# Moving Pool's sums, weight loads and mask operations in a fused attention and FFN block

## Chip, cores and metric

The kernel runs on one core of one Trainium2 chip. The metric is the device time of one execution in microseconds (us), as the median of several executions. Single executions of one kernel mostly agree to about 0.3%. The trace of a run is of one execution, which need not be a typical one.

TensorE is called PE, VectorE DVE, ScalarE ACT and GpSimd Pool. SP is the engine that here only issues DMA transfers, in program order.

## The reference

A pre-norm linear attention block is followed by a pre-norm gated FFN, on 2048 tokens of width 1024, in bf16:

```python
h  = x + A(layernorm(x))         # A: wqkv (1024 x 3072), 32 heads of 32
                                 # phi(t) = where(t > 0, t+1, exp(t)) + 1e-6
                                 # kv = sum_s phi(k) v ;  z = sum_s phi(k)
                                 # o = phi(q) kv / (phi(q) z + 1e-6) ;  out = o @ wo
h2 = h + B(layernorm(h))         # B: (relu(x Wg) * (x Wu)) @ Wd, F = 3584
```

## The kernel before

A token tile is 128 tokens, so there are 16. The program has four stretches:

1. **K and V, to about 140 us.** LN of each x tile, then k, v and their running product kv. From tile 4 on the products use Strassen's scheme with seven products in place of eight, which needs sums of weight blocks. Pool makes 32 of those: 16 for the V weights, then 16 for the Q weights.
2. **Q groups, 140 to 194 us.** In the first of them the kv sums are masked by head ("KV masks").
3. **Token tiles, 194 to 266 us.** For each tile: numerator `num`, quotient `o`, a DMA transpose of o, the o-projection, `h`, a store of h, LN on ACT and Pool, a DMA transpose of the normalized tile, and at the end four sums `S` over all eight tiles on DVE.
4. **FFN, 266 us to the end.** PE without a gap.

A buffer tracker turns every operation's reads and writes into semaphore waits, and each engine runs its operations in program order. That order is what the change alters. First, the Pool sums hang on the LN statistics: after a tile's rstd, up to three of them are issued.

```python
def ln_stats(src_full, src_chunk_bufs, name):
    # ... dve: bn_stats, bn_aggr, ve = var + eps
    PL.add("pool", lambda e: e.tensor_tensor(out=rstd[:, k, :], in0=ve[:, k, :], in1=neghalf[:], op=ALU.pow), ...)

def ln1_stats(st):
    ln1_k[st] = ln_stats(x1[:, i, :], B_x1[i], "ln1_%d" % st)
    for _ in range(min(3, len(pool_q))):
        pool_q.pop(0)()               # weight sums: TWv (16), then TWq (16)
```

The token tiles come from this loop. `a4` is the o-projection with h, the store of h and the first half of LN; `a4_norm` is LN's last step on ACT with the transpose; `a2` is numerator, quotient and the transpose of o.

```python
for _ in range(NWG):                  # NWG = 6
    load_w_next()                     # 512 KB of FFN weights each
LAG = NE                              # 4
for t in range(NE, NST + LAG + 1):
    if LAG + 1 <= t < TPP + LAG + 1:
        a4_norm(t - LAG - 1)          # ACT: xn = norm ; SP: transpose xn -> hnT
    if LAG <= t < NST + LAG:
        a4(t - LAG)                   # PE: o @ wo ; DVE: h ; SP: load x, store h
                                      # ACT, Pool: mean, variance, rstd (tiles 0 to 7)
    if t < NST:
        a2(t)                         # PE: num ; DVE: o = num / den ; SP: transpose o
    if t == 8:
        for f_ in t_sums(0, "pool") + t_sums(1, "pool"):
            f_()                      # eight Pool sums in a row
    if 13 <= t < 17:
        s_sums()[t - 13]()            # DVE: S sums, read all of hnT
```

h has three buffers (`NHS = 3`): h of tile t waits until tile t-3 has been normalized and its store has been read out.

## Time and profile before

The median is 778.93 us, and the profiled execution has a span of 777.3 us. Times inside a trace count from the start of its span. In the table, the first o-projection ends the Q groups, and the last numerator product (tile 15) is the last step of the token tiles at which PE waited in this kernel.

| | before |
|---|---|
| median of 4 | 778.93 us |
| products of tiles 14 and 15 into kv (end of K and V) | 139.81 us |
| first o-projection (first recorded matmul) | 194.31 us |
| last numerator product | 251.68 us |
| from there to the end | 525.6 us |

The page says that PE is 96% busy, but that average hides the start. These are its slices of the span (40 equal ones of 19.4 us; digits are tenths of busy time, PEclk tenths of the full clock that was granted):

```profile
PE   7698999999996999999999999999999999999998
...
DVE  5789976889755698888887656756686776753343
...
PEclk9799999999998999999999999999999999999999
```

PE's gaps are in the first 13 slices. After that come the last o-projections and the FFN, and nothing in this change touches them. Next, the timeline of Pool around 20 us: start, duration, engine, line, operation, result and inputs, count, and in brackets the idle time just before with what ended it.

```profile
20.40 3.60 POOL L725 TENSOR_TENSOR RW<-RAB 128x512 f16<-128x512 bf16 x3 [8.69 <-DMA RAB<-in_A_wqkv_dram]
23.96 0.55 POOL L613 TENSOR_TENSOR rstd<-ve,neghalf 128x1 f32<-128x1 f32 x1
24.48 3.67 POOL L725 TENSOR_TENSOR RW<-RAB 128x512 f16<-128x512 bf16 x3
```

Pool stood idle for 8.69 us because its first weight sum waited for a wqkv load. The rstd of tile 3 stands behind those three sums. This wait passes down the line, as the timelines of DVE and PE show (in PE's line `ps<-ident,RXH` is the transpose of tile 3's normalized x):

```profile
24.55 1.36 DVE L619 TENSOR_SCALAR RXH<-RE,mv,rstd 128x1024 bf16<-128x1024 bf16 x1 [8.87 <-POOL rstd L613]
```
```profile
25.97 1.04 PE L675 MATMUL ps<-ident,RXH 128*128 128x128 bf16 x8 [9.28 <-DVE RXH L619]
```

The same DVE line shows a second effect: the norm took 1.36 us beside a Pool sum. Alone it takes 0.54 us, as in the timeline of DVE at 37.96 us. Two 10 us windows show the stretch on either side of this wait: from 20 us on nobody but Pool is full, and from 80 us on DVE is the full engine, not PE. Columns: window, its length, busy us (and instructions) of PE, PEld, DVE, ACT and Pool, then granted clock, DMA share and GB/s.

```profile
20.00:30.00 10.00, 4.03 (x16) 2.05 (x17) 5.32 (x8) 1.08 (x2) 9.28 (x10) 0.50 0.09 30
...
80.00:90.00 10.00, 8.77 (x52) 4.14 (x52) 9.66 (x22) 3.96 (x7) 3.43 (x4) 1.00 0.36 80
```

In the token tiles, the waits in the window from 195 to 260 us (engine, line, what it waited for, us in total, times, longest) name Pool again. The eight sums in a row kept tile 5's LN back, ACT waited 7.4 us at one place, and DVE waited 5.8 us for a free h buffer:

```profile
ACT RXH L1033 <- POOL s L1023: 17.3, 8, 7.4
...
DVE RXH L994 <- ACT RXH L1033: 5.8, 1, 5.8
```

PE's timeline shows what came of it. `RW,RE` is an o-projection (16 matmuls, about 3.5 us), `kvz,RAB` a numerator. Some records are missing, hence 15 for 16.

```profile
231.64 3.63 PE L592 MATMUL ps<-RW,RE 128*128 128x512 bf16 x16 [1.07 <-DMA RE<-RE]
237.85 0.64 PE L592 MATMUL ps<-kvz,RAB 128*128 128x132 bf16 x8 [2.59 <-DVE RE L975]
241.26 5.58 PE L592 MATMUL ps<-RW,RE 128*128 128x512 bf16 x15 [2.77 <-DMA RE<-RE]
...
251.68 0.64 PE L592 MATMUL ps<-kvz,RAB 128*128 128x132 bf16 x8 [0.92 <-DVE RE L975]
```

An undisturbed tile takes 3.92 us. The projection at 241.26 us took 5.58 us because the clock had dropped to half in the stalls (granted 0.50 from 240 to 244 us).

### The profile page before, as it was taken

Reading aid. Unit: us, or ns where it says so; the run is one execution under the profiler, and the core shown is the slowest. Engines: PE = TensorE matmul, PEld = TensorE weight load, DVE = VectorE, ACT = ScalarE, POOL = GpSimd, SP = SyncE. Lnnn points to the kernel's source line nnn. Section 1 sums busy time; section 2 is a strip of 40 time slices with the busy share of each in tenths; the row PEclk is TensorE's granted clock in tenths of the full one; section 3 lists DMA queues with packets and bytes.
Section 4 is the critical chain, followed back from the end, with each engine's and each line's share of the span. In section 5 each row is a group of like instructions: output and inputs, shape, how many; then the busy total and the mean of one; then the engine's idle time right before and its main releaser. Section 6 shows DMA issues by size and latency. Waiting matters only on the chain.

```text
span 777.3 us, 10071 instructions
## 1 busy us (share of the span) xinstructions
PE 743.3 (96%) x3544; PEld 337.6 (43%) x3599; DVE 554.2 (71%) x1104; ACT 294.4 (38%) x502; POOL 75.6 (10%) x116
## 2 busy tenths in 40 slices
PE   7698999999996999999999999999999999999998
PEld 3343444334443444444444444444444444444443
DVE  5789976889755698888887656756686776753343
ACT  3234556566644145445454200014545445421000
POOL 1776200000261000000000010000000000000000
PEclk9799999999998999999999999999999999999999
DMA  9343210401997677655543799871322313026664
GB/s 304 118 120 82 55 28 1 148 6 37 279 209 196 209 222 237 188 166 164 178 147 114 240 245 270 250 249 55 109 86 77 109 55 108 1 61 183 203 183 142
DMA packets 160226, 113.39 MB, mean 146 GB/s; under 512 B 51504, under 2 KB 141360, under 8 KB 160176
## 3 DMA queue, kind: packets, MB, share of 16 engines
q1 hardware_dynamic: 160176, 112.75, 50.4%
q8 instruction: 28, 0.46, 0.2%
q14 instruction: 22, 0.18, 0.1%
HBM read 85.46 MB, written 15.73 MB: 130 GB/s over the span
## 4 chain that ended last, share of the span: by engine, by line
PE 75%; DVE 8%; ACT 6%; POOL 5%; issue 4%; DMA 2%; SPq 0%; DVEq 0%; POOLq 0%; ACTq 0%
PE ps L592 75%; POOL RW L725 2%; ACT ps L597 1%; DVE st L605 1%; DMA RAB<-in_A_wqkv_dram 1%; POOL RO L1088 1%; ACT RX L630 1%; DVE RX L634 1%; DVE RXH L619 1%; ACT RX L1010 1%; ACT RX L1007 1%; DVE RX L826 1%; DVE RAB L637 1%; POOL rstd L613 1%; ACT RXH L597 1%
## 5 line engine op out<-in xcount | busy, mean ns | idle before, releaser
L592 PE MATMUL ps<-RC,RO 128*128 128x512 f16 x672 | 154.2, 379 | 0.0
L597 ACT ACTIVATE ps<-ps 128x512 f32<-128x512 f32 x152 | 88.7, 583 | 169.7 <-PE ps L592 158.3
L592 PE MATMUL ps<-RW,RAB 128*128 128x512 f16 (+1 forms) x685 | 151.1, 379 | 0.6
L592 PEld LDWEIGHTS ps<-RW,RAB 128*128 128x128 bf16 (+1 forms) x696 | 68.1, 98 | 82.2
L592 PE MATMUL ps<-RH,RWG 128*128 128x512 bf16 x435 | 103.0, 379 | 0.7
L592 PEld LDWEIGHTS ps<-RC,RO 128*128 128x128 f16 x672 | 65.7, 98 | 79.3
L597 ACT ACTIVATE RE<-ps 128x512 f32<-128x512 f32 x120 | 71.0, 597 | 76.7 <-PE ps L592 54.5
L592 PE MATMUL ps<-RC,RWG 128*128 128x512 f16 x296 | 70.7, 379 | 0.0
L1157 DVE TENSOR_TENSOR RAB<-ps,RAB 128x512 bf16<-128x512 f32 x28 | 19.4, 692 | 67.1 <-PE ps L592 66.8
L592 PEld LDWEIGHTS ps<-RH,RWG 128*128 128x128 bf16 x448 | 43.8, 98 | 52.9
L592 PE MATMUL ps<-RW,RE 128*128 128x512 bf16 x248 | 58.8, 389 | 5.2 <-DMA RE<-RE 4.2
L592 PE MATMUL ps<-RH,RO 128*128 128x512 bf16 (+1 forms) x242 | 58.3, 379 | 0.7
L597 ACT ACTIVATE RAB<-ps 128x512 bf16<-128x512 f32 x56 | 33.4, 597 | 62.1 <-PE ps L592 62.1
L592 PE MATMUL ps<-RAB 128*128 128x512 bf16 x215 | 53.6, 390 | 1.3 <-ACT RAB L678 0.7
L1088 DVE TENSOR_TENSOR RO<-RWG,RO 128x512 f16<-128x512 bf16 x108 | 45.4, 420 | 1.8
L592 PEld LDWEIGHTS ps<-RC,RWG 128*128 128x128 bf16 (+1 forms) x296 | 28.5, 98 | 35.7 <-ACT ps L597 2.2
L1164 DVE TENSOR_TENSOR RE<-ps,RE 128x512 f32<-128x512 f32 x56 | 38.5, 691 | 5.1 <-ACT RE L597 5.0
L613 POOL TENSOR_TENSOR rstd<-ve,neghalf 128x1 f32<-128x1 f32 x24 | 14.6, 610 | 281.6 <-DVE ve L610 281.6
L1088 DVE TENSOR_TENSOR RO<-RWG 128x512 f16<-128x512 bf16 x108 | 40.6, 417 | 0.0
L605 DVE BATCH_NORM_STATS2 st<-RE 128x6 f32<-128x512 bf16 x48 | 30.7, 681 | 13.7 <-DMA RE<-h_scr 12.8
L592 PEld LDWEIGHTS ps<-RW,RE 128*128 128x128 bf16 x256 | 24.7, 100 | 34.6 <-DMA RE<-RE 5.2
L1169 DVE TENSOR_TENSOR RE<-ps,RE 128x512 f32<-128x512 f32 x56 | 38.2, 681 | 0.0
(111 smaller groups left out, 796.3 us busy)
## 6 DMA issues: line engine op xcount, KB each, us to landing
RWG<-in_B_W_gate_dram SPq DMA_DIRECT2D x28, 512.0 KB, 3.7
RWG<-in_B_W_up_dram SPq DMA_DIRECT2D x28, 512.0 KB, 4.9
RW<-t_scr SPq DMA_DIRECT2D x56, 256.0 KB, 3.3
RW<-in_B_W_down_dram SPq DMA_DIRECT2D x42, 256.0 KB, 4.4
RE<-in_A_x_dram SPq DMA_DIRECT2D x31, 256.0 KB, 3.6
RW<-in_B_W_down_dram SPq DMA_DIRECT2D x14, 512.0 KB, 3.9
t_scr<-RW SPq DMA_DIRECT2D x14, 512.0 KB, 4.9
RAB<-in_A_wqkv_dram SPq DMA_DIRECT2D x8, 512.0 KB, 8.3
```

The source lines that it names most:

```text
L592: lambda e: e.matmul(out_ap, lhsT, rhs, start=start, stop=stop, skip_group_check=skip),
L597: PL.add("act", lambda e: e.activation(out=dst, in_=src, func=func), reads=reads, writes=writes, name=name)
L605: PL.add("dve", lambda e, c=c: e.bn_stats(out=st6[:, k, c * 6:(c + 1) * 6], in_=src_full[:, c * BCH:(c + 1) * BCH]), reads=[src_chunk_bufs ...
L613: PL.add("pool", lambda e: e.tensor_tensor(out=rstd[:, k, :], in0=ve[:, k, :], in1=neghalf[:], op=ALU.pow), reads=[B_ve[k], B_neghalf], wr ...
L619: PL.add("dve", lambda e: e.tensor_scalar(out=dst_ap, in0=src_full, scalar1=mv[:, k, 0:1], scalar2=rstd[:, k, :], op0=ALU.subtract, op1=AL ...
L630: PL.add("act", lambda e: e.activation(out=Et[:, k, :], in_=src, func=ACTF.Exp), reads=[src_buf], writes=[B_E[k]], name=name + "_exp")
L634: PL.add("dve", lambda e: e.tensor_scalar(out=Et[:, k, :], in0=Et[:, k, :], scalar1=1.0, scalar2=1e-6, op0=ALU.min, op1=ALU.add), reads=[] ...
L725: PL.add(eng, lambda e: e.tensor_tensor(out=tw(j)[:, d0:d0 + chunk, :], in0=in0(d0), in1=in1(d0), op=ALU.subtract), reads=reads, writes=[b ...
L1088: PL.add(eng, lambda e: e.tensor_tensor(out=Tring[:, k, j], in0=in0, in1=in1, op=ALU.subtract), reads=reads, writes=[B_T[k][j]], name="T%d ...
L1157: PL.add("dve", lambda e: e.tensor_tensor(out=hh[:, f1, 0:SBW], in0=bank(BA[1]), in1=r11[:, rr, :], op=ALU.mult), reads=[B_bank[BA[1]], B_ ...
L1164: PL.add("dve", lambda e, w=w: e.tensor_tensor(out=ftmp[:, 4 + w, :], in0=bank(BF_[w]), in1=ftmp[:, 2 + w, :], op=ALU.add), reads=[B_bank[ ...
L1169: PL.add("dve", lambda e, w=w: e.tensor_tensor(out=ftmp[:, 6 + w, :], in0=bank(BB[w]), in1=ftmp[:, w, :], op=ALU.add), reads=[B_bank[BB[w] ...
```

## The change

The intent has three parts. The weight sums start only at tile 5, so that no LN step stands behind a sum that waits for a load. The eight FFN sums of Pool go one per tile, and the six FFN weight loads one per tile too, from tile 5 to tile 10, so that they don't all come at once. The 24 small KV mask operations become five wide ones, two Q groups later.

```diff
         def ln1_stats(st):
             ln1_k[st] = ln_stats(x1[:, i, :], B_x1[i], "ln1_%d" % st)
-            for _ in range(min(3, len(pool_q))):
-                pool_q.pop(0)()
+            run(pool_q, {5: 5, 6: 5, 7: 3, 8: 3, 9: 2, 10: 2}.get(st, 3) if st >= 5 else 0)
 ...
         def kvfin():
-            for g in range(NG):       # 8 x: kvz[g] = kv[g] * bmask
-            for g in range(NG):       # 8 x: zsb[g] = one column of PSUM
-            for g in range(NG):       # 8 x: kvz[g, P:] = bmask4 * zsb[g]   (bodies cut)
+            for b0, nb, ng, g0 in ((0, 2, GPB, 0), (2, 1, NG - 2 * GPB, 2 * GPB)):
+                # kvm: one tensor_tensor over nb*ng groups, mask broadcast (cut)
+                # zsb: one tensor_copy over nb*ng groups (cut)
+            PL.add("dve", lambda e: e.tensor_tensor(
+                out=kvz[:, :, P:P + HPG], in0=bmask4[:].unsqueeze(1).to_broadcast([P, NG, HPG]),
+                in1=zsb[:].unsqueeze(2).to_broadcast([P, NG, HPG]), op=ALU.mult), ...)
 ...
                 if r == 0 and ct == 0:
-                    hooks[3] = lambda: (kvacc(NST - 2), kvacc(NST - 1), kvfin())
+                    hooks[3] = lambda: (kvacc(NST - 2), kvacc(NST - 1))
+                if r == 0 and ct == 2:
+                    hooks[3] = kvfin
 ...
         flush()
-        for _ in range(NWG):
-            load_w_next()
         LAG = NE
+        pool_t = t_sums(0, "pool") + t_sums(1, "pool")
         for t in range(NE, NST + LAG + 1):
             ...
-            if t == 8:
-                for f_ in t_sums(0, "pool") + t_sums(1, "pool"):
-                    f_()
+            if 5 <= t < 5 + NWG:
+                load_w_next()
+            if t >= 9:
+                run(pool_t, 1)
```

## The prediction

It was made from the kernel before, its trace and the diff alone, before the changed kernel had been built.

> **What bounds it now.** By the chain of waits, TensorE work is 75% of the 777.3 us span. From about 266 us on (the FFN) TensorE is busy throughout; the change leaves that alone. The time to win lies in the first 254 us.
>
> **1. Weight sums on Pool.** *Now:* the first three sums stand on Pool in front of tile 3's rstd and wait 8.69 us for a wqkv load (timeline of Pool, 20.40 us). VectorE waits 8.87 us for that rstd and TensorE 9.28 us for VectorE's norm; afterwards the granted clock is 0.50 (20 to 30 us). After the change no sum precedes tile 5, so this goes. But from 30 to 96 us VectorE is 95 to 98% busy in most windows and sets the pace, so the slow clock is hidden. And the sums cost VectorE: a norm takes 0.54 us alone and 1.36 us beside a Pool sum, an L634 step 0.28 against 0.6 to 1.05. The Trainium skill ("SBUF — State Buffer", Who interferes with whom) says VectorE and GpSimd share a port pair as an exclusive lock; these durations agree. I count about 12 us so lost, some 0.45 us per sum. Today 3 of the 32 sums fall in the idle gap; then all will fall in busy time, and tiles 12 to 14 get 9 instead of 2, where VectorE has little slack. Estimate: +8.9 (wait gone) + 0.8 (its inflated norm) - 1.4 (more collisions) = **8.3 us gained**.
>
> **2. KV masks.** 24 small VectorE operations take 4.3 us (140.65 to 144.9 us) in the first Q group; TensorE loses 0.76 + 0.70 us. Five wide ones, estimated from 0.69 us for 512 and 1.22 us for 1024 elements out of PSUM: 1.9 us, two groups later. **1.1 us gained.**
>
> **3. Token tiles.** *Now:* eight Pool sums (222.5 to 231.65 us) stand in front of tile 5's LN steps; ACT waits 7.4 us for Pool, VectorE 5.8 us for a free h buffer, TensorE 1.07 + 2.59 + 2.77 + 0.92 us, in part at clock 0.50. The o-projection of tile 12 starts at 252.15 us; at the undisturbed 3.92 us per tile it would be 241.4. One sum per tile fits into Pool's 2.46 us gap. But LN repeats only every 4.885 us on ACT and Pool, its transposes stand in SP's order before the next o transposes (landing 4.2 us): tile 12 can't start before about 245.2. Then VectorE's S sums wait for tile 7's transpose and hold o of tile 14: about 247.5. The six spread 512 KB weight loads take SP's issue time (0.6 to 1.4 us each) and DMA time (share above 1.0 from 198 to 230 us) from these transposes, while the idle DMA before 195 us goes unused. **4.0 us gained** (0 to 7).
>
> **Sum:** 8.3 + 1.1 + 4.0 = 13.4: **765.5 us** (1.7% less), range 760.5 to 770.5. Faster by over 2%: 0.29; within 2%: 0.69; slower: 0.02.
>
> **To check:** no TensorE wait for VectorE's norm near 17 us and no half clock there; Pool sums between 22 and 95 us, VectorE nearly full; K group of tiles 4 and 5 about 11 us earlier, shrinking to 8 by 100 us; masks under 2 us; LN every 4.9 us without the 7.4 us hole; a wait of 2 to 4 us before the last numerator product, behind the S sums.
>
> **What would make it wrong:** bursts of five sums colliding more (gain 5) or mostly with idle VectorE (gain 11); transposes queueing behind the spread loads; the second stall dropping TensorE's clock.

## The result, and the profile after

The changed kernel takes 770.81 us (770.62 to 771.08, 4 runs) against 778.93 us. The ratio is 0.9896, with a 95% interval from 0.9879 to 0.9913. Ratios are the mean time of one kernel's fast runs over that of the other's in the same rounds, so they aren't quite the ratio of the medians. The gain is 8.1 us; 13.4 were predicted. The time lies just above the range.

| | before | after | gain in this stretch |
|---|---|---|---|
| end of K and V | 139.81 | 131.79 | 8.02 |
| first o-projection | 194.31 | 184.97 | 1.32 |
| last numerator product | 251.68 | 243.40 | -1.06 |
| end of the span | 777.3 | 769.0 | 0.0 |

The first two stretches gained what was forecast (8.3 and 1.1 us). The third was to gain 4.0 us and lost one. The lines of the changed kernel are numbered 3 or 4 higher than before.

In the slices of the page, each now 19.2 us long, PE's weak start is gone from the first two slices (8 and 9 where there was 7 and 6) and DVE is fuller there. The third slice has become weaker (7 where there was 9): it holds the wait of 4.7 us for DVE shown below. At the token tiles the one dip of PE to 6 (13th slice) has become two slices of 7 (12th and 13th):

```profile
PE   8979999999977999999999999999999999999998
...
DVE  7989975889746698888886756748676686653433
...
PEclk9989999999999999999999999999999999999999
```

The timeline of Pool shows the rstd of tiles 3 and 4 free of any sum, and the first five sums behind tile 5's:

```profile
14.91 0.55 POOL L613 TENSOR_TENSOR rstd<-ve,neghalf 128x1 f32<-128x1 f32 x1 [3.15 <-DVE ve L610]
17.98 0.55 POOL L613 TENSOR_TENSOR rstd<-ve,neghalf 128x1 f32<-128x1 f32 x1 [2.53 <-DVE ve L610]
21.91 0.55 POOL L613 TENSOR_TENSOR rstd<-ve,neghalf 128x1 f32<-128x1 f32 x1 [3.38 <-DVE ve L610]
22.43 6.14 POOL L728 TENSOR_TENSOR RW<-RAB 128x512 f16<-128x512 bf16 x5
```

PE's transpose of tile 3 comes at 16.58 instead of 25.97 us, without a wait. What remains: in the table of PE's waits, the one for DVE's phi step in the K group of tiles 4 and 5 has grown from 2.2 to 4.7 us, and the largest is now for transposes of o:

```profile
PE ps L592 <- DMA RE<-RE: 8.0, 5, 3.1
PE ps L592 <- DVE RE L637: 4.7, 1, 4.7
...
PE ps L592 <- DVE RE L979: 1.4, 1, 1.4
```

The five mask operations take 1.6 us (146.76 to 148.40 us) by the timeline of DVE, where the 24 took 4.3 (140.65 to 144.92 us); first the kernel before, then the changed one:

```profile
140.65 1.67 DVE L941 TENSOR_TENSOR kvz<-ps,bmask 128x128 bf16<-128x128 f32 x8 [1.50 <-PE ps L592]
142.24 1.49 DVE L947 COPY zsb<-ps 128x1 f32<-128x1 f32 x8
143.77 1.15 DVE L950 TENSOR_SCALAR kvz<-bmask,zsb 128x4 bf16<-128x4 f32 x8
```
```profile
146.76 0.95 DVE L946 TENSOR_TENSOR kvz<-ps,bmask 128x768 bf16<-128x768 f32 x1
147.63 0.15 DVE L950 COPY zsb<-ps 128x6 f32<-128x6 f32 x1
147.70 0.41 DVE L946 TENSOR_TENSOR kvz<-ps,bmask 128x256 bf16<-128x256 f32 x1
148.03 0.15 DVE L950 COPY zsb<-ps 128x2 f32<-128x2 f32 x1
148.21 0.19 DVE L953 TENSOR_TENSOR kvz<-bmask,zsb 128x32 bf16<-128x32 f32 x1
```

In the token tiles the waits have changed their names. The longest wait of ACT for Pool is 1.4 us where it was 7.4, so the sums are indeed out of the way. Now DVE waits for the stores of h (four times, 11.2 us), PE for transposes of o, and DVE's first S sum for the last transpose of LN:

```profile
ACT RXH L1037 <- POOL s L1027: 11.4, 8, 1.4
DVE RXH L998 <- DMA h_scr<-RXH: 11.2, 4, 4.4
...
PE ps L592 <- DMA RE<-RE: 8.0, 5, 3.1
...
DVE RC L1074 <- DMA RH<-RXH: 4.7, 1, 4.7
```

SP's timeline shows where they come from. First one tile of the kernel before, then the changed kernel. Each tile has a transpose of o (`RE<-RE`), now a weight load (`RWG<-in_B_W...`), then the LN transpose (`RH<-RXH`), a load of x and a store of h. The second column is how long SP was busy issuing:

```profile
217.97 1.43 SPq L502 DMA_TRANSPOSE RE<-RE  x1
219.45 1.66 SPq L502 DMA_TRANSPOSE RH<-RXH  x1
```
```profile
221.37 1.47 SPq L502 DMA_TRANSPOSE RE<-RE  x1
222.88 0.58 SPq L498 DMA_DIRECT2D RWG<-in_B_W_gate_dram  x1
223.51 3.43 SPq L502 DMA_TRANSPOSE RH<-RXH  x1
...
228.15 1.47 SPq L502 DMA_TRANSPOSE RE<-RE  x1
229.67 0.58 SPq L498 DMA_DIRECT2D RWG<-in_B_W_up_dram  x1
230.29 2.48 SPq L502 DMA_TRANSPOSE RH<-RXH  x1
```

The LN transpose behind a weight load took 3.43 and 2.48 us to issue; before, its median was 1.35 us. Everything behind it in SP's order comes later. ACT finished tile 7's norm at 229.2 us; its transpose was issued at 235.49 us, 6.3 us later. So LN's own pace (4.885 us per tile, kept exactly) no longer set the pace of the tiles; the transfers behind SP's queue did.

### The profile page after: what moved, and what is told of

It is laid out like the page before. It is cut to its first block, busy times and chain, and to the rows that moved or that the text cites. A ratio compares the mean times of both kernels' runs of the same rounds, so it can differ in the third digit from the quotient of the medians.

```text
span 769.0 us, 10054 instructions
## 1 busy us (share of the span) xinstructions
PE 741.7 (96%) x3544; PEld 337.4 (44%) x3599; DVE 553.2 (72%) x1085; ACT 294.2 (38%) x502; POOL 75.9 (10%) x116
## 4 chain that ended last, share of the span: by engine, by line
PE 79%; DVE 8%; ACT 5%; issue 3%; DMA 2%; POOL 2%; SPq 1%; DVEq 0%; ACTq 0%; POOLq 0%
PE ps L592 79%; DVE RX L634 1%; ACT RX L1014 1%; ACT RX L1011 1%; ACT ps L597 1%; DMA RE<-in_A_x_dram 1%; DVE RE L637 1%; ACT RX L630 1%; DVE st L605 1%; DVE RX L829 1%; SPq L498 1%; DVE RAB L637 1%; DVE RC L728 1%; DMA RE<-RE 1%; DVE RXH L619 1%
## 5 line engine op out<-in xcount | busy, mean ns | idle before, releaser
L597 ACT ACTIVATE RE<-ps 128x512 f32<-128x512 f32 x120 | 71.0, 597 | 76.7 <-PE ps L592 54.5
L592 PEld LDWEIGHTS ps<-RH,RWG 128*128 128x128 bf16 x448 | 43.8, 98 | 52.9
L605 DVE BATCH_NORM_STATS2 st<-RE 128x6 f32<-128x512 bf16 x48 | 30.7, 680 | 13.9 <-DMA RE<-h_scr 12.9
```

The costliest lines, as they stand in the source:

```text
L592: lambda e: e.matmul(out_ap, lhsT, rhs, start=start, stop=stop, skip_group_check=skip),
L597: PL.add("act", lambda e: e.activation(out=dst, in_=src, func=func), reads=reads, writes=writes, name=name)
L605: PL.add("dve", lambda e, c=c: e.bn_stats(out=st6[:, k, c * 6:(c + 1) * 6], in_=src_full[:, c * BCH:(c + 1) * BCH]), reads=[src_chunk_bufs ...
```

## The experiments

Twelve kernels ran. All outputs are right. **Theory D** is that the spread loads delay the transposes and stores which the tiles wait for, in SP's queue and on the DMA engines. **Rival L** is that LN's pace and the place of the S sums bound the token tiles, whatever the loads do. Later runs ask two more things: what part of D is issue time and what part is bytes, and whether Pool's sums really cost DVE time.

| run | median us | ratio to before (95%) | first o-proj. | last num. | tiles, us |
|---|---|---|---|---|---|
| before | 778.93 | 1 | 194.31* | 251.68 | 57.6 |
| changed | 770.81 | 0.9896 (0.9879 to 0.9913) | 184.97* | 243.40 | 58.7 |
| loads_front | 763.5 | 0.9807 (0.9792 to 0.9821) | 185.58* | 238.27 | 52.9 |
| spread_only | 779.64 | 1.001 (0.9997 to 1.0022) | 194.38* | 252.09 | 57.9 |
| tilesums_only | 773.95 | 0.9934 (0.9921 to 0.9946) | 193.90* | 245.47 | 51.8 |
| wsums_only | 770.3 | 0.9888 (0.9873 to 0.9903) | 185.68* | 243.00 | 57.5 |
| front_issue | 765.75 | 0.9829 (0.9815 to 0.9844) | 183.70 | 237.87 | 54.2 |
| two_front_four_late | 764.98 | 0.9817 (0.9803 to 0.9832) | 184.46 | 236.29 | 51.8 |
| front_wq_sums_late | 768.72 | 0.9865 (0.985 to 0.988) | 188.27 | 241.19 | 52.9 |
| front_norm_later | 768.14 | 0.986 (0.9843 to 0.9876) | 184.20 | 237.52 | 53.3 |
| norm_later_s_later | 759.72 | 0.9761 (0.9748 to 0.9774) | 183.87 | 231.31 | 47.4 |
| wq_sums_paced | 768.17 | 0.9861 (0.9848 to 0.9875) | 188.32 | 240.10 | 51.8 |
| masks_old_place | 762.78 | 0.9792 (0.9779 to 0.9806) | 183.13 | 234.91 | 51.8 |
| combined | 762.25 | 0.9789 (0.9772 to 0.9806) | 189.82 | 236.40 | 46.6 |

The last three columns are from each run's one profiled execution. "Tiles" is the difference of the two times before it; where a star stands, the first of the 16 matmuls has no record, and its 0.22 us has been added. The edits below are cut to their main lines. Those of loads_front and two_front_four_late are against the changed kernel, those of the three runs ending in "only" against the kernel before, that of norm_later_s_later is against front_norm_later, and the others are against loads_front.

### loads_front: the changed kernel, loads in one block again

```diff
@@ -1430,6 +1430,8 @@
                     for i in range(NX2):
                         load_x2(i)
         flush()
+        for _ in range(NWG):
+            load_w_next()
         LAG = NE
         pool_t = t_sums(0, "pool") + t_sums(1, "pool")
         for t in range(NE, NST + LAG + 1):
@@ -1439,8 +1441,6 @@
                 a4(t - LAG)
             if t < NST:
                 a2(t)
-            if 5 <= t < 5 + NWG:
-                load_w_next()
             if t >= 9:
                 run(pool_t, 1)
             if 13 <= t < 17:
```

> The changed kernel with the six FFN weight loads put back in one block ahead of the token tiles. Theory D (the spread loads hold up the o and LN transposes and the h stores in SP's queue and on the DMA engines): 765.7 us, 5 us less than the changed kernel's 770.8; no VectorE wait for an h store over 2 us, tile 7's LN transpose issued within 2 us of its norm (6.3 us in the changed kernel), o-projection of tile 12 some 5 us earlier. Rival L (LN's pace of 4.885 us and the S sums bound the stage by themselves): 770 to 771 us.

Measured: 763.5 us (762.76 to 765.93), 7.3 us less than the changed kernel; the tiles take 52.9 instead of 58.7 us. Tile 7's transpose was issued 0.2 us after its norm's end (229.85 and 230.00 us). DVE still waited once 2.5 us for an h store, a little over what was expected. PE's waits for transposes of o fell from 8.0 to 2.9 us. Rival L falls: it allowed no gain. And the whole time fell by more than the 5.8 us of the tiles, within the scatter of this kernel's four runs (3.2 us). The trace is of the slowest of the four. Of the other kernels with no load beside the LN tiles and LN's order as it was, four took 51.8 us for the tiles and one 52.9, so the loads' cost is 5.8 to 6.9 us.

What PE's timeline says of the tiles here is close to what the prediction had worked out without a charge for the loads:

```profile
238.27 0.64 PE L592 MATMUL ps<-kvz,RAB 128*128 128x132 bf16 x8 [1.89 <-DVE RE L979]
238.75 6.42 PE L592 MATMUL ps<-RW,RE 128*128 128x512 bf16 x28
```

Tile 12's projection begins at 238.75 us, 53.2 us after the first one. Before, that distance was 57.84 us. The gain is 4.7 us; the prediction had 4.0. In the kernels with 51.8 us the tiles gain 5.8.

### spread_only: the kernel before, loads spread

```diff
@@ -1428,8 +1428,6 @@
                     for i in range(NX2):
                         load_x2(i)
         flush()
-        for _ in range(NWG):
-            load_w_next()
         LAG = NE
         for t in range(NE, NST + LAG + 1):
             if LAG + 1 <= t < TPP + LAG + 1:
@@ -1438,6 +1436,8 @@
                 a4(t - LAG)
             if t < NST:
                 a2(t)
+            if 5 <= t < 5 + NWG:
+                load_w_next()
             if t == 8:
                 for f_ in t_sums(0, "pool") + t_sums(1, "pool"):
                     f_()
```

> The kernel before with one edit: the six loads spread over tiles 5 to 10. Theory D: slower than before, 780 to 783 us (part of the 5 us hides in the 7.4 us hole that the block of Pool sums still makes at tile 9, in which the DMA engines catch up). Rival L: 779 us.

Measured: 779.64 us, ratio 1.001 (0.9997 to 1.0022): no difference beyond noise, and less than theory D had expected (780 to 783). The waits are all there, 11.1 us of DVE for h stores and 8.7 us of PE for transposes, nearly as in the changed kernel. They cost nothing in the end, because, as SP's timeline suggests, the block of Pool sums still held LN back: at tile 5 to 7 the transposes were issued within 0.1 us of their norms again, so SP had caught up in Pool's hole. By itself this run can't tell D from L; together with loads_front it says that the cost of the spread loads shows only once Pool's block is gone.

### tilesums_only: the kernel before, Pool's eight sums one per tile

```diff
@@ -1431,6 +1431,7 @@
         for _ in range(NWG):
             load_w_next()
         LAG = NE
+        pool_t = t_sums(0, "pool") + t_sums(1, "pool")
         for t in range(NE, NST + LAG + 1):
             if LAG + 1 <= t < TPP + LAG + 1:
                 a4_norm(t - LAG - 1)
@@ -1438,9 +1439,8 @@
                 a4(t - LAG)
             if t < NST:
                 a2(t)
-            if t == 8:
-                for f_ in t_sums(0, "pool") + t_sums(1, "pool"):
-                    f_()
+            if t >= 9 and pool_t:
+                pool_t.pop(0)()
             if 13 <= t < 17:
                 s_sums()[t - 13]()
         for q in range(NWR):
```

> The kernel before with one edit: the eight Pool sums one per token tile from tile 9 on, loads still in a block. Theory D, with the prediction's estimate for the token tiles standing where the loads are not spread: 774 to 775 us, the 7.4 us wait of ACT for Pool gone, tile 12's o-projection at about 247.5 in place of 252.15 us. Rival L: no gain, 778 to 779 us.

Measured: 773.95 us (772.8 to 775.35), and tile 12's projection at 245.95 us; the tiles take 51.8 instead of 57.6 us. So this part alone is worth 5 to 6 us, if the loads stay in their block.

### wsums_only: the kernel before, weight sums from tile 5 on

```diff
@@ -656,7 +656,8 @@
         def ln1_stats(st):
             i = st % NX1
             ln1_k[st] = ln_stats(x1[:, i, :], B_x1[i], "ln1_%d" % st)
-            for _ in range(min(3, len(pool_q))):
+            n_ = {5: 5, 6: 5, 7: 3, 8: 3, 9: 2, 10: 2}.get(st, 3) if st >= 5 else 0
+            for _ in range(min(n_, len(pool_q))):
                 pool_q.pop(0)()
 
         def ln1_norm(st):
```

> The kernel before with one edit: Pool's 32 weight sums after the LN steps of tiles 5 to 14 instead of 2 to 12. From the two traces this part is worth 8.0 us (start of the Q groups 139.8 against 131.8 us): 770.9 us. If the parts of the change help each other (a later stage that uses the earlier start better or worse) it is off by more than 1 us.

Measured: 770.3 us (770.1 to 770.41). This one edit gives as much as the whole change. With it the accounts close: alone, the parts are worth -8.6 (weight sums), -5.0 (tile sums) and +0.7 us (loads), and the masks -1.3 us by the traces. Added up that is -14.2 us; the change brought -8.1. The missing 6 us is the clash of two parts that are each harmless alone: the loads cost 0.7 us (within noise) beside Pool's block and 7.3 us (763.5 to 770.81) once the tile sums are spread.

### front_issue: small transfers at the places of the spread loads

```diff
@@ -1441,6 +1441,10 @@
                 a4(t - LAG)
             if t < NST:
                 a2(t)
+            if 5 <= t < 5 + NWG:
+                i_ = t - 5
+                dma(sl_w[i_], wring[:, i_, 0, :], (wg_v if i_ % 2 == 0 else wu_v)[:, 0, (i_ // 2) * 2 * P:(i_ // 2 + 1) * 2 * P],
+                    "again_%d" % i_, writes=[B_w[i_]])
             if t >= 9:
                 run(pool_t, 1)
             if 13 <= t < 17:
```

> Loads in a block ahead of the tiles (763.5 us), plus six more SP transfers at the places of the spread loads, each an eighth of one weight load (64 KB, the same data again). Separates SP's issue time from the bytes on the DMA engines. If the bytes of the spread loads, queued ahead of the transposes, were the cost: 763.5 to 765 us. If the extra issues in SP's order were: 767 us or more, towards the changed kernel's 770.8.

Measured: 765.75 us (765.51 to 766.08), at the upper edge of what the byte reading allowed and below what the issue reading asked for. The tiles take 54.2 us: 1.3 us more than in loads_front, and 2.4 more than in other runs with the loads in a block (51.8). The changed kernel has 5.8 to 6.9 more. SP's timeline shows the difference. A small transfer takes as long to issue as a full load (0.58 us), but the LN transpose right behind it is issued in 1.24 to 1.28 us in five cases of six:

```profile
205.62 0.58 SPq L498 DMA_DIRECT2D RWG<-in_B_W_up_dram  x1
206.24 1.27 SPq L502 DMA_TRANSPOSE RH<-RXH  x1
```

So most of the cost goes with the 512 KB in front of the transposes, and about a quarter to a third with the issue and the small transfer. The run doesn't divide those two. In SP's own time, the LN transposes of tiles 1 to 6 took 15.0 us to issue in the changed kernel, 10.9 in loads_front, where no load stands between, and 9.0 here; the six additional issues took 3.8 and 3.5 us. How long a transpose takes to issue thus varies with what is queued before it, from 1.24 to 3.43 us in these three runs. That the bytes lengthen it fits these sums; why they do is not shown.

### two_front_four_late: loads kept away from the LN tiles

```diff
         flush()
+        for _ in range(2):
+            load_w_next()
         LAG = NE
...
-            if 5 <= t < 5 + NWG:
+            if 13 <= t < 17:
                 load_w_next()
```

> The changed kernel with the first two weight loads ahead of the tiles and the other four at tiles 13 to 16, after the last LN transpose. If it is only the overlap with the LN tiles that costs: 762 to 764 us, as good as all six ahead (the transposes of tiles 4 to 6 start sooner, those of 13 to 15 a little later). If any load among the tiles costs its 1.5 us of DMA time: about 766 us.

Measured: 764.98 us (764.07 to 765.36), between the two expectations; the tiles take 51.8 us, as short as with all loads ahead. Four loads among tiles 13 to 16, where no LN transpose comes any more, cost nothing that the tiles show. Spreading by itself isn't the fault, then; the place is. Against loads_front of another chip the ratios (0.9817 and 0.9807) don't differ beyond their intervals.

### front_wq_sums_late and wq_sums_paced: the Q weights' sums later

In the trace before, the sums cost DVE time. The norm and the small steps of phi (L634) are 0.54 and 0.28 us alone and up to 1.37 and 1.05 us beside Pool sums. Adding up what such operations take beyond their undisturbed durations, from 15 to 135 us, gives 13.8 us before and 15.4 us after, so the change added 1.6 us (1.4 had been predicted). The next two runs tried to move 16 of the sums to a place where DVE has more room.

```diff
-            run(pool_q, {5: 5, 6: 5, 7: 3, 8: 3, 9: 2, 10: 2}.get(st, 3) if st >= 5 else 0)
+            run(pool_q, {5: 5, 6: 5, 7: 3, 8: 3, 15: 16}.get(st, 0))          # front_wq_sums_late
```

> Loads ahead of the tiles (763.5 us), and the 16 sums for the Q weights all after tile 15 instead of after tiles 9 to 14. If the sums cost VectorE time where it sets the pace (0.4 to 0.5 us each, port shared with Pool): the K groups' 10 to 11 us lead is kept to 100 us, 760.5 to 761.5 us. If the lead is lost for another reason (the bound is VectorE's own work): 763 to 764 us.

Measured: 768.72 us, 5 us slower than loads_front, against both expectations. While the 16 sums ran on Pool (91.59 to 112 us), PE waited 2.98 and 1.70 us for ACT, whose longest waits there were for DVE, and the clock was at half from 100.93 to 104.35 us. The second try sent them in pairs, each pair waiting for the DVE operation issued last:

```diff
+        def sums_now(n):
+            pace[:] = PL.prog["dve"][-1:]      # the sums get this as a dependency
+            run(pool_q, n)
 ...
             def h_v5(p=p):
+                if p >= 5:
+                    sums_now(2)                # likewise in four other hooks, from group 5 or 6 on
```

> The loads ahead of the tiles (763.5 us), and the 16 sums for the Q weights in twos between 95 and 125 us, each pair made to wait for a VectorE operation, in place of 16 in a row after tile 15 (768.7 us) or of tiles 9 to 14. If the row of 16 was slow because it met VectorE's work one after the other: 761 to 762 us, K groups of tiles 8 and 9 about 2.5 us earlier and nothing lost later. If a sum costs 0.45 us of TensorE time wherever it stands: 763 to 765 us.

Measured: 768.17 us, no better. The first half of the reasoning held: in wq_sums_paced the kv products between two K groups come at 61.48 and 101.94 us, 40.46 us apart, against 42.72 (62.69 and 105.41 us) in loads_front. That is 2.3 us gained by taking the sums out. Then it was lost, and more. The pairs met DVE's own sums of x (L760), which take both operands from SBUF: 0.42 us alone, 1.26 us beside a Pool sum.

```profile
110.57 2.67 DVE L760 TENSOR_TENSOR RWG<-RAB 128x512 f16<-128x512 bf16 x2
113.27 1.26 DVE L760 TENSOR_TENSOR RWG<-RWG,RAB 128x512 f16<-128x512 f16 x1
114.56 1.26 DVE L760 TENSOR_TENSOR RH<-RAB,RWG 128x512 f16<-128x512 bf16 x1
...
119.37 0.42 DVE L760 TENSOR_TENSOR RH<-RAB,RWG 128x512 f16<-128x512 bf16 x1
```

The next line of PE's timeline in the same run is the consequence: ACT waited 4.6 us for the DVE step behind these sums (L896 at 115.74 us), and PE for ACT. Two 4 us windows show the sequel (granted clock 0.69, then 0.50):

```profile
117.09 1.51 PE L592 MATMUL ps<-RC,RWG 128*128 128x512 f16 x4 [2.41 <-ACT ps L597]
```
```profile
116.00:120.00 4.00, 2.38 (x12) 1.30 (x12) 3.93 (x6) 1.09 (x2) 2.41 (x2) 0.69 0.00 0
120.00:124.00 4.00, 3.54 (x15) 1.87 (x16) 0.53 (x2) 1.68 (x3) 3.31 (x3) 0.50 0.01 4
```

PE waited 2.41 us, ran at half clock from 117.5 us on (0.69 over the window of 116 to 120 us means half clock for its last 2.5 us), and waited another 0.99 us. Neither of the two places tried was free for Pool's sums; what a sum cost depended on which DVE operation stood beside it.

### front_norm_later and norm_later_s_later: LN's order

LN takes 4.885 us per tile because ACT waits 1.4 us for Pool's rstd before it normalizes, with the next tile's sums behind it.

```diff
@@ -1435,12 +1435,12 @@
         LAG = NE
         pool_t = t_sums(0, "pool") + t_sums(1, "pool")
         for t in range(NE, NST + LAG + 1):
-            if LAG + 1 <= t < TPP + LAG + 1:
-                a4_norm(t - LAG - 1)
             if LAG <= t < NST + LAG:
                 a4(t - LAG)
             if t < NST:
                 a2(t)
+            if LAG + 1 <= t < TPP + LAG + 1:
+                a4_norm(t - LAG - 1)
             if t >= 9:
                 run(pool_t, 1)
             if 13 <= t < 17:
```

> Loads ahead of the tiles (763.5 us), and each tile's normalization on ACT issued after the next tile's two sums and after the o product, so that ACT doesn't stand idle while Pool makes rstd and SP issues the o transpose first. If LN's 4.885 us per tile bounds the token tiles: LN falls to 3.9 to 4.1 us per tile, tile 7's LN transpose comes 4 us sooner, 760 to 761 us. If the DMA engines bound them (about 4 us of DMA time per tile): 762.5 to 763.5 us.

Measured: 768.14 us, slower. The LN part came out as wanted: ACT's norms follow each other every 3.92 us, as PE's tiles do. But DVE, in its order, now reached the first S sum long before the transpose of tile 7 had landed:

```profile
DVE RC L1074 <- DMA RH<-RXH: 6.3, 1, 6.3
PE ps L592 <- DVE RE L979: 5.8, 1, 5.8
```

PE stood 5.8 us and came back at half clock: the numerator behind the wait took 1.06 us where 0.63 is usual, and 52 of the projections' matmuls 13.9 us. The remedy is to issue the S sums two tiles later.

```diff
@@ -1443,8 +1443,8 @@
                 a4_norm(t - LAG - 1)
             if t >= 9:
                 run(pool_t, 1)
-            if 13 <= t < 17:
-                s_sums()[t - 13]()
+            if 15 <= t < 19:
+                s_sums()[t - 15]()
         for q in range(NWR):
             load_wraw(q)
         wt_at = {0: [0], 1: [1, 2], 2: [3, 4]}
```

> The loads ahead of the tiles and the normalization issued later, as in the run with the norm later (768.1 us), and VectorE's four S sums two tiles later (tiles 15 to 18). There LN kept pace (3.9 us per tile) but VectorE stood at the first S sum for 6.3 us and TensorE then 5.8 us at half clock. If that order was all that spoiled it: no VectorE wait over 2 us for tile 7's transpose, o-projection of tile 12 at about 231.5 us, 757 to 759 us. If the DMA engines bound the tiles anyway: 762 us or more.

Measured: 759.72 us (759.54 to 762.27), ratio 0.9761. The tiles take 47.4 us, that is 3.95 us for each of the twelve, next to PE's own 3.92. PE no longer waits before the last numerator, and tile 12's projection starts at 231.78 us:

```profile
231.31 0.63 PE L592 MATMUL ps<-kvz,RAB 128*128 128x132 bf16 x8
```

No wait of DVE for tile 7's transpose is left. This is the fastest kernel, and it beats both the kernel before (by 19 us) and the changed one (by 11).

### masks_old_place: wide, not moved

```diff
                 if r == 0 and ct == 0:
-                    hooks[3] = lambda: (kvacc(NST - 2), kvacc(NST - 1))
-                if r == 0 and ct == 2:
-                    hooks[3] = kvfin
+                    hooks[3] = lambda: (kvacc(NST - 2), kvacc(NST - 1), kvfin())
```

> The loads ahead of the tiles (763.5 us), with the five wide mask operations back in the first Q group. Separates wide from moved: the part is worth 1.3 us by the traces (Q groups 54.5 against 53.2 us). If the width does it: 763.5 to 763.9 us. If the move does it: 764.5 to 764.8 us.

Measured: 762.78 us (762.57 to 762.87). This is a little below both expectations and nearer to the first: the width does it; the move brings nothing that these runs could show. In the old place the five operations took 1.6 us as well, and PE doesn't wait there. In all four kernels with the 24 small operations PE waits 0.76 + 0.70 us there, and the Q groups take 54.5 us; in none with the five wide ones it does.

### combined

This kernel has two loads ahead and four late, the norm and S sums later, and the paced pairs of Q weight sums.

> All that the runs speak for: two loads ahead and four at tiles 13 to 16, normalization later, S sums later, Q weight sums in paced pairs. If the gains add: 755 to 757 us. If the paced pairs bring nothing: 757 to 759 us.

Measured: 762.25 us (760.77 to 765.15, 5 runs), no better than norm_later_s_later alone and against both expectations. In the trace, which is of the slowest of the five, the tiles are the shortest of all (46.6 us), but the first o-projection comes at 189.8 us, late as in wq_sums_paced, and PE waits the same 2.4 us for ACT. So in that execution the paced pairs spoil it.

## Why the prediction was wrong

**Weight sums: right.** Predicted 8.3 us, measured 8.02 in the changed kernel and 8.6 alone. K and V end between 130.6 and 132.4 us in the eight kernels with this order of the sums, so one trace is good to about 1 us here. The wait behind the wqkv load went, DVE set the pace next, and the additional collisions cost 1.6 us. The collisions agree with the Trainium skill ("SBUF — State Buffer", Who interferes with whom): a DVE operation in a two-port mode contends with a Pool operation, and one with two SBUF inputs with a Pool operation that reads SBUF. The trace doesn't record the mode, but it shows slow operations of both shapes: the norm, with one SBUF tensor as input, goes from 0.54 to 1.37 us, and the sum of x with two SBUF inputs from 0.42 to 1.26 us. A phi step (L637) with one operand in PSUM keeps its 0.69 us beside Pool sums.

The 11.46 us lead at the K group of tiles 4 and 5 (40.01 against 51.47 us) had shrunk to 8.0 by the Q groups, as forecast.

**Masks: right.** Predicted 1.1 us, measured 1.32, and masks_old_place shows that the width brings it. That the move helps was never shown.

**Token tiles: wrong, by 5 us.** The failing step is the prediction's item 3. It said: "The six spread 512 KB weight loads take SP's issue time (0.6 to 1.4 us each) and DMA time (share above 1.0 from 198 to 230 us) from these transposes". It then charged them with next to nothing. It took 247.5 us from LN's order and the S sums, which is a gain of 4.65 us on 252.15, and put down 4.0, so at most 0.65 us is left for the loads. The loads cost 5.8 us (58.7 against 52.9 us in loads_front), or 6.9 against the runs with 51.8. Without them the same sum was good to 0.7 us against loads_front, and to 1.8 us against the others.

The mechanism had been named, once more under what would make the prediction wrong ("transposes queueing behind the spread loads"), and its size left out. It could have been worked out from the trace before: DMA was full from 198 to 230 us (but for one 2 us window at a share of 0.72), with 19 tile transfers of 256 KB taking the 20 us from 208 to 228, about 4.2 us of DMA time per tile of four. Six loads at the 340 GB/s of the block would add about 1.5 us each, 9 us in all, where LN left 0.7 us of room per tile (4.885 - 4.2), 4 us in all. The difference is 5 us. That is an estimate after the fact, and it fits.

The Trainium skill says the same in general ("DMA: Bandwidth & Descriptors", Issuing engines are not separate DMA queues): all transfers run on the same 16 DMA engines and interleave, and the time to issue a transfer "is usually small relative to the DMA itself". The run front_issue agrees for the loads: six issues with an eighth of the bytes cost 1.3 to 2.4 us, the full loads 5.8 to 6.9. For a transpose the issue is not so small here: 1.3 to 1.7 us in the kernel before (208 to 228 us), against a median of 3.6 to 4.2 us from issue to landing.

**The second stall and the clock: named, and seen elsewhere.** In the changed kernel the last numerator waited only 1.38 us. But another stall halved its clock, from 220.98 to 224.39 us: PE had waited 3.09 us for tile 8's transpose of o, and the projection took 5.31 us. It doesn't show in the time: an execution with a mean clock of 0.998, which leaves room for only one such stretch in all, took 770.89 us. In front_norm_later the wait was 5.8 us, and the granted clock fell.

The Trainium skill ("TensorE: Matmul & The Clock Gate", What's actually happening) gives about 3.4 us as the window after which an idle PE is halved. The traces agree on the window: within each of the 14, clock changes lie whole multiples of 3.41 us apart. But the window need not be idle throughout. In wq_sums_paced one wait of 2.41 us was enough: PE was busy for 1.00 of the 3.41 us before the drop at 117.51 us. Cut into such windows from 7 us on, the 14 traces show a drop after every full-clock window in which PE was busy for up to 1.34 us (front_norm_later, 45.39 to 48.80 us), and none after a window with 1.45 us or more (wsums_only, 224.67 to 228.08 us); the ends of matmuls are modelled, so these two figures are rough.

**What stays open:** how the 1.3 to 2.4 us of front_issue divides between SP's time and the small transfers' own DMA time, and why bytes in front of a transpose lengthen its issue. The early stretch also came out 1 to 2 us apart in eight kernels that don't differ there. The clock goes with it: after PE's wait of 4.1 to 4.7 us in the K group of tiles 4 and 5, it was at half for one window (3.41 us) in five of the traces and for two in the other three, and the next kv products come at 60.2 to 61.0 us in the five and at 61.3 to 62.7 us in the three.

## What to carry to other kernels

Before you spread transfers "to even out the load", look at what they will stand in front of: on one queue that runs in order, a load that nobody needs yet delays every transpose and store behind it. Here that cost 5.8 us or more beside the LN transposes, and nothing that could be seen after the last of them. Taking one bottleneck away shows the next; the spread loads were free as long as Pool's block hid them, so price each part of a change with the others already in place. When small work is moved to another time on a neighbour that slows an engine down, as Pool's sums did DVE, ask which operations it will run beside, not only how busy the engine is on average.

## What the Trainium skill lacked or had wrong

- "DMA: Bandwidth & Descriptors" doesn't say that the issue of a DMA transpose itself is held up on the issuing engine when a large load is queued just ahead: 1.24 to 1.28 us in five cases of six behind 64 KB, 1.9 to 3.4 us behind 512 KB (SP's timelines of front_issue and of the changed kernel). Other backlogs do it too: 1.4 to 3.0 us in loads_front with no load just ahead.
- The same page gives an effective rate for DMA transposes but not what a mixed stream reaches: loads, stores and SBUF-to-SBUF transposes of 256 KB together moved about 240 GB/s at a DMA share above 1.0, where plain weight loads moved 340.
- "SBUF — State Buffer" says that the port lock blocks fully, and the durations here fit that. No page gives a price to plan with: here a Pool sum of about 1.2 us cost DVE 0.43 us on average (13.8 us over 32 sums), and 0.8 us in the norm (0.54 to 1.37 us) or in an operation with two SBUF inputs (0.42 to 1.26 us).
- "TensorE: Matmul & The Clock Gate" has the halved clock follow an idle window of about 3.4 us. Here the window need not be idle: the clock was halved after windows with PE busy for up to 1.34 of 3.41 us, and one wait of 2.41 us was enough (wq_sums_paced).
